# Key stage of a packed attention kernel: exponentials transposed by VectorE instead of TensorE, values loaded in long runs, the value products split into 32x32 tiles

## The chip, the cores and the metric

The kernel runs on one core of a Trainium2 chip. The metric is the device time of one execution in microseconds (us). Before the change the median of three runs was 1665.73 us (1664.1 to 1666.33). TensorE (PE) multiplies matrices into PSUM, VectorE (DVE), ScalarE (ACT) and GpSimd (POOL) do elementwise work, and SyncE (SP) issues all DMAs here. Each engine works through its own instructions in order and waits on semaphores.

## The reference, cut to what matters

```python
def sm_attn(qq, kk, vv):                      # scale = 1/sqrt(64)
    s = scale * np.matmul(qq, kk.transpose(0, 1, 3, 2))
    s = s - np.max(s, axis=-1, keepdims=True)
    a = np.exp(s)
    a = a / (np.sum(a, axis=-1, keepdims=True) + 1e-09)
    return np.matmul(a, vv)
p_packed = sm_attn(p, k, v)                   # p: (8, 8, 32, 64); k, v: (8, 8, 576, 64)
out = sm_attn(q, p_packed, p_packed)          # q: (8, 8, 576, 64)
x = out.transpose(0, 2, 1, 3).reshape(4608, 512)
# then RMS norm, a gated layer (512 -> 1536 -> 512) and a layer with g = h*cos(h) (512 -> 2048 -> 512)
```

For each of 8 batches and 8 heads, 32 latent rows p attend to 576 keys and values. Their result is the key and the value of a second attention, whose queries are q. The change lies in the first attention alone.

## The kernel before, in words

The first attention is called the key stage here. It takes 16 groups, one after the other: a group i is four heads of one batch, so 4 heads x 32 latents fill the 128 partitions. The loop over i (L621 to L672, 18 rounds) is written as a software pipeline, and its order is the engines' order: it stands under a manual schedule. In round i these helpers follow each other:

- `u_et(i-1)` transposes the exponentials of the group before: six TensorE transposes `et` (L431), two ScalarE copies to `eT` (L432), and on VectorE the sum's reciprocal (L434, L435).
- `u_s1(i)` multiplies latents and keys into the scores `s` (L404, from group 11 on L408); VectorE takes the maximum `mx` (L412) and scales it (L413).
- `u_prep(i+1)` transposes the next latents (`pt`, L376) and copies them to `pT` on VectorE (L377); `u_kt(i+1, ...)` transposes the next keys (`kp`, L389), copied by ScalarE to `kT` (L392).
- `u_fin(i-2)` transposes the result `cd` of two groups before (`tp`, L459), ScalarE copies it to `tf` (L461), VectorE writes `ppT` (L464).
- `u_e(i)` takes the exponentials `e` on ScalarE (L420).
- `w_prep(n, 0)` and later `w_late` narrow 64-bit float weights to 32 bits: an absolute value on ScalarE (L133) and then four VectorE operations (L143, L145, L149, L153) per weight tile; "the narrowing" below means these four. One or two tiles are due in a round. `wo_split` (L528, L531) divides such a tile into a high and a low part.
- `u_pp(i-1)` multiplies `eT` with the values `vn` into `pp` (L445, 24 products: six chunks of keys by four heads), and VectorE evicts them to `cd` (L449), scaled by the reciprocal. `cd` has two buffers; the stores of `cd` and `tf` go to DRAM at the start of the next round (`store`, L578).
- `bg0_step` drives pieces of the second attention of batch 0 from round 5 on (`qtp`, `sp`, `st`, `amx`, `at`, `xp`, `ssq`, `rp`), and `unit` (rounds 6, 10, 14) multiplies narrowed weights `wy` with `ppT` into `mps` (L565), split by `hilo` (L106, L107) into `wmhl`.

Keys come in one DMA for each group, with 4608 contiguous bytes for each partition, values in three (L360), each to 32 partitions, for each of these four heads with runs of 1536 bytes. `vn` has three buffers with a zeroed border (L336, L618); `e` has a border too (L339). After the loop the core goes over to the gated layer (`gv`, L158 to L160), whose first product waits for the pieces `apt` of the second attention.

Of the kernel before, what the change touches and what calls it, by code (L numbers as in the profile page):

```python
# [9 lines left out]
F32 = mybir.dt.float32  # L10
F32R = mybir.dt.float32r
I32 = mybir.dt.int32
AF = mybir.ActivationFunctionType
# [7 lines left out]
def kernel(  # L21
# [14 lines left out]
    nc = tc.nc  # L36
    B, H, S, D = q.shape
    NP = p.shape[2]
# [3 lines left out]
    CP = 96  # L42
    NC_ = S // CP
    HALF = S // 2
    CH = NC_ // 2
# [4 lines left out]
    NG = 2 * B  # L50
# [9 lines left out]
    BG_B, KP_B = 2, 4  # L60
    WO_U = 4
    REST = S - 512
    V_P = 16
    R_LOAD, R_SPLIT, S_AT = (1, 2), (4, 5), (20, 21, 24 + 1, 24 + 2)
    W_FROM, W_TO = 1, 16
    W_ORD = (0, 1, 2, 3, 16, 4, 5, 6, 17, 7, 8, 18, 9, 10, 11, 19, 12, 13, 14)
# [7 lines left out]
    B0_W = (15, 16, 17, 18, 19, -4, 20, 21, -5, 22, 23, -6, 0, -7, 0, -8, 0, -9, 0, -10, 0, -11)  # L74
    B0_L, B0_LEAD = {15: (0,), 16: (1, 2), 17: (3,)}, 4
    W_LOAD, W_SPLIT = (4, 6, 14, 16), (9, 11, 17, 19)
    W2_I0, W2_POOL = 28, False
    T_END, F3_B, OWN = 2, 3, 16
    LAG, LAG_B = 3, 4
# [12 lines left out]
    ident = const.tile([128, 128], F32, name="ident")  # L92
# [87 lines left out]
    u5 = ust.enter_context(tc.tile_pool(name="u5", bufs=4))  # L180
    u2 = ust.enter_context(tc.tile_pool(name="u2", bufs=2))
    u1 = ust.enter_context(tc.tile_pool(name="u1", bufs=1))
    ps_2 = pst.enter_context(tc.tile_pool(name="ps_2", bufs=KP_B, space=PSUM))
# [5 lines left out]
    pT = u1.tile([128, 4, 160], F32, name="pT")  # L189
# [22 lines left out]
    def att_load(b):  # L212
        nc.sync.dma_start(out=bq, in_=q_dram[b])
# [117 lines left out]
                fs[word[0]](int(word[1]), int(word[2]))  # L331
            yield nxt[:1]

    v_t = [u2.tile([128, 4, NC_, D], F32, tag=f"vn{x}", name="vn", bufs=1) for x in range(3)]
    for x in range(2):
        nc.vector.memset(v_t[x], 0.0)  # L336
    e_pad = u2.tile([128, 2 * V_P + S], F32, tag="e", name="e", bufs=1)
    for x in (slice(0, V_P), slice(V_P + S, 2 * V_P + S)):
        nc.vector.memset(e_pad[:, x], 0.0)  # L339
    nat_k, nat_v = {}, {}  # L340
    st = {}

# [10 lines left out]
    def load_v(i):  # L353
        if i >= NG:
            return
        b, g = divmod(i, 2)
        vn = nat_v[i] = v_t[i % len(v_t)]
        vs = v[b, 4 * g:4 * g + 4].rearrange("h (p m c) d -> m p h c d", m=CH, c=NC_)
        for m in (0, 2, 1):
            nc.sync.dma_start(out=vn[V_P + m * 32:V_P + (m + 1) * 32], in_=vs[m])  # L360

    load_k(0)
    for i in range(2):
# [7 lines left out]
    def u_prep(i):  # L371
        pn, kn = nat_k.pop(i)
        z = st[i] = {}
        nc.gpsimd.tensor_copy(pn[:, 1], pn[:, 0])
        pt = ps_2.tile([128, 128], F32, tag="kp", name="pt")
        nc.tensor.transpose(pt, pn.rearrange("p a d -> p (a d)"), ident)  # L376
        nc.vector.tensor_copy(pT[:, :, :NP], pt.rearrange("p (h n) -> p h n", h=4))  # L377
        z["kT"], z["kn"] = u1.tile([128, 4, HALF], F32, tag="kT", name="kT"), kn

    def u_kt(i, ms):  # L380

        z = st[i]
        kT, kn = z["kT"], z["kn"]
        kv = kT.rearrange("q h (t m p) -> q h t m p", t=CH, m=CH)
        for m in ms:
            kp = ps_2.tile([128, CH * 128], F32, tag="kp", name="kp")
            for t in range(CH):
                r = 2 * (CH * m + t)
                nc.tensor.transpose(  # L389
                    kp[:, t * 128:(t + 1) * 128], kn[:, r:r + 2, :].rearrange("p c d -> p (c d)"), ident  # L390
                )
            nc.scalar.activation(  # L392
                out=kv[:, :, :, m, :], in_=kp.rearrange("q (t h p) -> q h t p", t=CH, h=4), func=AF.Copy
            )

    def u_s1(i):
# [19 lines left out]
    def u_e(i):  # L416
        z = st[i]
        s1, mx = z["s1"], z["mx"]
        e = e_pad[:, V_P:V_P + S].rearrange("p (a s) -> p a s", a=2)
        nc.scalar.activation(  # L420
            out=e, in_=s1[:, :, :HALF], func=AF.Exp, scale=scale, bias=mx[:, 1:2], accum_out=mx[:, 2:3]
        )

    def u_et(i):
        z = st[i]
        eT = u2.tile([128, NC_, 128], F32, tag="eT", name="eT", bufs=1)
        for hf in range(2):
            et = ps_2.tile([128, CH, 128], F32, tag="kp", name="et")
            for c in range(CH):
                cc = hf * CH + c  # L430
                nc.tensor.transpose(et[:, c, :], e_pad[:, cc * CP:cc * CP + 128], ident)  # L431
            nc.scalar.activation(out=eT[:, hf * CH:(hf + 1) * CH], in_=et, func=AF.Copy)  # L432
        z["eT"], mx = eT, z["mx"]
        nc.vector.tensor_scalar(out=mx[:, 2:3], in0=mx[:, 2:3], scalar1=1e-9, scalar2=None, op0=ALU.add)  # L434
        nc.vector.reciprocal(out=mx[:, 3:4], in_=mx[:, 2:3])  # L435

    def u_pp(i):
        b, g = divmod(i, 2)
        z = st[i]
        eT, vn, mx = z["eT"], nat_v.pop(i), z["mx"]  # L440
        pp = ps_2.tile([128, D], F32, tag="kp", name="pp")
        for c in range(NC_):
            for h in range(4):
                r = slice(h * NP, (h + 1) * NP)
                nc.tensor.matmul(  # L445
                    pp[r], eT[:, c, r], vn[:, h, c % CH * 2 + c // CH, :], start=c == 0, stop=c == NC_ - 1
                )
        cd = u2.tile([128, 2, D], F32, tag="cd", name="cd", bufs=2)
        nc.vector.tensor_scalar(  # L449
            out=cd, in0=pp.unsqueeze(1).to_broadcast([128, 2, D]), scalar1=mx[:, 3:4], scalar2=None, op0=ALU.mult  # L450
        )
        stores.append((c_dram[b][:, g, :], cd[:, 0, :]))
        z["cd"] = cd

    def u_fin(i):
        z = st[i]
        b, g = divmod(i, 2)
        tp = ps_2.tile([128, 4, NP], F32, tag="kp", name="tp")
        nc.tensor.transpose(tp.rearrange("p h n -> p (h n)"), z["cd"].rearrange("p a d -> p (a d)"), ident)  # L459
        tf = u2.tile([128, 4, NP], F32, tag="tf", name="tf", bufs=3)  # L460
        nc.scalar.activation(out=tf, in_=tp, func=AF.Copy)  # L461
        stores.append((q_dram[b][:, 4 * g:4 * g + 4, :], tf))
        n, t = b % 4, ppT[b // 4]
        nc.vector.tensor_tensor(  # L464
            out=t[:, 4 * g:4 * g + 4, n * NP:(n + 1) * NP], in0=tp,
            in1=gT[:, 4 * g:4 * g + 4].unsqueeze(2).to_broadcast([128, 4, NP]), op=ALU.mult
        )
        st.pop(i)
# [4 lines left out]
    def w_load(n):  # L473
        if n >= W_KV:
            wo_load(n - W_KV)
            return
        wy_load(n)
# [57 lines left out]
    def b0_load(x):  # L535
        if x < len(B0_W) and B0_W[x]:
            n = B0_W[x]
            (wy_load if n >= 0 else wo_load)(abs(n))
# [36 lines left out]
    def store(keep):  # L575
        while len(stores) > keep:
            dst, src = stores.pop(0)
            nc.sync.dma_start(out=dst, in_=src)  # L578
# [23 lines left out]
    def w_due(i):  # L602
        a, b = (n_w * max(0, min(x, W_TO) - W_FROM) // (W_TO - W_FROM) for x in (i, i + 1))
        return [W_ORD[x] for x in range(a, b)]
# [10 lines left out]
    order.enter_context(tc.manual_schedule())  # L615
    u_prep(0)
    u_kt(0, range(CH))
    nc.gpsimd.memset(v_t[2], 0.0)  # L618
    w_q, wo_q = [], []
    w_late = lambda: None  # L620
    for i in range(NG + 2):  # L621
        due = list(w_due(i))
        for n in due:
            w_load(n)
        load_k(i + 4)
        for n in B0_L.get(i, ()):
            b0_load(n)
        if i == 1:
            load_q()
            load_q()  # L630
        store(0)
        if i == U_ATT:
            att_load(0)
            att_load_c(0)
        if 0 < i <= NG:
            u_et(i - 1)
        if i < NG:
            u_s1(i)
        if i + 1 < NG:
            u_prep(i + 1)  # L640
            u_kt(i + 1, [0, 1])
        if 1 < i:
            u_fin(i - 2)
        if i <= NG:
            w_late()
        if i < NG:
            u_e(i)
        if i + 1 < NG:
            u_kt(i + 1, [2])
        for n in w_q:  # L650
            w_prep(n, 0)
        for n in wo_q:
            wo_split(n - W_KV, 0)
        bg0_step(i, 1)
        if 0 < i <= NG:
            u_pp(i - 1)
        if i in U_S:
            unit(0, U_S[i])
        bg0_step(i, 0 if i == U_ATT else 2)
        w_last = w_late  # L660

        def w_late(ns=tuple(w_q), os=tuple(wo_q)):
            for n in ns:
                w_prep(n, 1)
            for n in os:
                wo_split(n - W_KV, 1)
        if i < NG:
            w_late()
            w_late = lambda: None
        wo_q = [n for n in w_q if n >= W_KV]  # L670
        w_q = due
        load_v(i + 2)  # L672
# [187 lines left out]
    for i in range(len(seq) + LAG):  # L860
        b, f, hf = seq[min(i, len(seq) - 1)]
        j = i - b * B1
        if i < len(seq):
# [11 lines left out]
            t = gv_block(b, hf, f)  # L875
# [137 lines left out]
    for i in range(len(seq) + LAG_B):  # L1013
        if i < len(seq):
            n, f = seq[i]
# [16 lines left out]
        if LAG_B <= i < len(seq) + LAG_B - T_END:  # L1032
            n, f = seq[i - LAG_B]
# [33 lines left out]
```

## Time and profile before

| What | Before |
|---|---|
| Median of 3 runs | 1665.73 us |
| Profiled execution, its own time | 1664.63 us |
| Its span (first to last instruction) | 1662.8 us |
| TensorE busy over the span | 1607.7 us (97%) |
| VectorE, ScalarE, GpSimd busy | 1006.9, 809.6, 74.9 us |
| Mean granted TensorE clock | 0.983 |

The span is cut by the page into 40 slices of 41.6 us. TensorE is busy 7, 7, 6 and 7 tenths in the first four and 9 or 8 tenths in every later one; the DMA engines are busy 9 tenths or more in the first three. The key stage is what fills these four slices: the first product of the gated layer starts at 155.63 us. In the profile a product of 32-bit floats shows as two records, so 24 products `pp` are 48 records.

### The profile page before, as it was taken

Reading aid. Unit: us, or ns where it says so; the run is one execution under the profiler, and the core shown is the slowest. Engines: PE = TensorE matmul, PEld = TensorE weight load, DVE = VectorE, ACT = ScalarE, POOL = GpSimd, SP = SyncE. Lnnn points to the kernel's source line nnn. Section 1 sums busy time; section 2 is a strip of 40 time slices with the busy share of each in tenths; the row PEclk is TensorE's granted clock in tenths of the full one; section 3 lists DMA queues with packets and bytes.
Section 4 is the critical chain, followed back from the end, with each engine's and each line's share of the span. In section 5 each row is a group of like instructions: output and inputs, shape, how many; then the busy total and the mean of one; then the engine's idle time right before and its main releaser. Section 6 shows DMA issues by size and latency. Waiting matters only on the chain.

```text
span 1662.8 us, 25654 instructions
## 1 busy us (share of the span) xinstructions
PE 1607.7 (97%) x9920; PEld 1308.2 (79%) x9920; DVE 1006.9 (61%) x1890; ACT 809.6 (49%) x1519; POOL 74.9 (5%) x74
## 2 busy tenths in 40 slices
PE   7767989999999999999999999999999999999998
PEld 5545768787888888888988888888888888888887
DVE  3567985666666656564426665656565656565554
ACT  3455554444454444443425555545454545454443
POOL 1000540000000000000210000000000000000000
PEclk9787999999999999999999999999999999999999
DMA  9996754454645453533372110101010101000001
GB/s 235 266 268 198 227 165 153 155 189 145 198 140 185 147 196 131 169 125 110 112 257 77 38 38 1 51 1 51 1 51 0 51 1 51 1 10 16 1 26 26
DMA packets 103577, 177.31 MB, mean 107 GB/s; under 512 B 39456, under 2 KB 55840, under 8 KB 103456
## 3 DMA queue, kind: packets, MB, share of 16 engines
q1 hardware_dynamic: 103456, 175.68, 34.9%
q8 instruction: 78, 1.28, 0.3%
q14 instruction: 43, 0.35, 0.1%
HBM read 134.22 MB, written 41.42 MB: 106 GB/s over the span
## 4 chain that ended last, share of the span: by engine, by line
PE 89%; DVE 4%; DMA 3%; ACT 1%; issue 1%; POOL 0%; SPq 0%; DVEq 0%; ACTq 0%; POOLq 0%
PE hp L159 8%; PE hp L160 8%; PE hp L158 8%; PE ops L160 8%; PE ops L159 8%; PE ops L158 8%; PE gv L158 6%; PE acc L158 6%; PE gv L159 6%; PE acc L160 6%; PE gv L160 6%; PE acc L159 6%; PE mps L565 3%; DMA c<-cd 2%; PE qtp L229 1%
## 5 line engine op out<-in xcount | busy, mean ns | idle before, releaser
L158 PE MATMUL gv<-apt,wmhl 128*128 128x288 f32 x768 | 234.0, 305 | 2.0 <-ACT apt L106 0.9
L159 PE MATMUL gv<-apt,wmhl 128*128 128x288 f32 x768 | 227.8, 297 | 0.4 <-DVE apt L107 0.4
L160 PE MATMUL gv<-apt,wmhl 128*128 128x288 f32 x768 | 226.8, 295 | 0.0
L159 PE MATMUL hp<-xhl,wmhl 128*128 128x512 f32 x576 | 224.1, 389 | 0.0
L160 PE MATMUL hp<-xhl,wmhl 128*128 128x512 f32 x576 | 224.1, 389 | 0.0
L158 PE MATMUL ops<-w2hl,ghl 128*128 128x512 f32 x576 | 224.1, 389 | 0.0
L159 PE MATMUL ops<-w2hl,ghl 128*128 128x512 f32 x576 | 224.1, 389 | 0.0
L158 PE MATMUL hp<-xhl,wmhl 128*128 128x512 f32 x576 | 223.9, 389 | 0.0
L160 PE MATMUL ops<-w2hl,ghl 128*128 128x512 f32 x576 | 222.3, 389 | 0.0
L966 ACT ACTIVATE r<-r 128x512 f32<-128x512 f32 x144 | 91.0, 632 | 250.0 <-DVE r L965 250.0
L974 DVE TENSOR_TENSOR r<-r,hp 128x512 f32<-128x512 f32 x144 | 98.9, 687 | 164.7 <-ACT r L967 164.7
L758 ACT ACTIVATE shl<-silu 128x288 fp32r<-128x288 f32 x192 | 85.4, 445 | 201.6 <-DVE silu L751 201.6
L158 PEld LDWEIGHTS gv<-apt,wmhl 128*128 128x128 f32 x768 | 145.0, 189 | 49.0 <-issue 15.3
L158 PE MATMUL acc<-shl,wohl 128*128 128x512 f32 x432 | 175.4, 406 | 1.1 <-ACT wohl L528 0.9
L160 PE MATMUL acc<-shl,wohl 128*128 128x512 f32 x432 | 170.4, 394 | 2.8 <-POOL wohl L531 2.8
L159 PE MATMUL acc<-shl,wohl 128*128 128x512 f32 x432 | 169.6, 393 | 0.0
L961 ACT ACTIVATE kk<-hp,magic 128x512 f32<-128x512 f32 x144 | 99.1, 688 | 117.4 <-PE hp L160 117.2
L751 DVE TENSOR_TENSOR silu<-silu,gv 128x288 f32<-128x288 f32 x192 | 86.4, 450 | 106.8 <-PE gv L160 81.9
L159 PEld LDWEIGHTS gv<-apt,wmhl 128*128 128x128 f32 x768 | 145.0, 189 | 5.9 <-DVE apt L107 0.6
L160 PEld LDWEIGHTS gv<-apt,wmhl 128*128 128x128 f32 x768 | 144.9, 189 | 0.0
L962 DVE TENSOR_SCALAR kk<-kk 128x512 f32<-128x512 f32 x144 | 61.4, 426 | 116.2 <-ACT kk L961 116.1
L159 PEld LDWEIGHTS ops<-w2hl,ghl 128*128 128x128 f32 x576 | 108.2, 188 | 22.6
(122 smaller groups left out, 2624.6 us busy)
## 6 DMA issues: line engine op xcount, KB each, us to landing
wy<-wy SPq DMA_DIRECT2D x96, 512.0 KB, 4.6
kn<-in_k_dram SPq DMA_DIRECT2D x16, 576.0 KB, 7.9
vn<-in_v_dram SPq DMA_DIRECT2D x48, 192.0 KB, 6.7
qnat<-in_q_dram SPq DMA_DIRECT2D x32, 288.0 KB, 4.1
x_dram<-x SPq DMA_DIRECT2D x18, 512.0 KB, 3.0
x1raw<-x_dram SPq DMA_DIRECT2D x18, 512.0 KB, 3.9
raw<-in_moe_w_in_dram SPq DMA_DIRECT2D x16, 512.0 KB, 4.3
raw<-in_moe_w_out_dram SPq DMA_DIRECT2D x16, 512.0 KB, 4.3
```

The costliest lines, as they stand in the source:

```text
L158: nc.tensor.matmul(ps, lhi, rhi, start=first, stop=False)
L159: nc.tensor.matmul(ps, lhi, rlo, start=False, stop=False)
L160: nc.tensor.matmul(ps, llo, rhi, start=False, stop=last)
L229: nc.tensor.transpose(tp[:, c * CP:(c + 1) * CP], qv[:, i, 2 * c:2 * c + 2, :].rearrange("p c d -> p (c d)"), ident[:CP, :CP],)
L565: nc.tensor.matmul(ps[kt][h * NP:(h + 1) * NP], ppT[b // 4][rows, 4 * kt + h, n:n + NP], w_y[2 * u + kt][rows, j], start=True, stop=True,)
L751: nc.vector.tensor_tensor(out=t, in0=t, in1=pss[1], op=ALU.mult)
L758: nc.scalar.activation(out=sh[:, 0, cols], in_=t, func=AF.Copy)
L961: nc.scalar.activation(out=kk, in_=hp, func=AF.Identity, scale=1.0 / TWO_PI, bias=magic[:, 0:1])
L962: nc.vector.tensor_scalar(out=kk, in0=kk, scalar1=-MAGIC, scalar2=None, op0=ALU.add)
L966: nc.scalar.activation(out=r, in_=r, func=AF.Abs)
L974: nc.vector.tensor_tensor(out=r, in0=r, in1=hp, op=ALU.mult)
```

## The change

Five things are changed, all in the key stage.

1. The exponentials are no longer transposed by TensorE with ScalarE copies: one VectorE instruction turns the 32x32 blocks of `e` into `eT`.
2. The order of keys within a group changes with it: `kT` takes the keys so that a chunk is 32 keys of one head in that head's 32 partitions. Values come in the layout of the keys: one DMA for each group, 128 partitions, 4608 contiguous bytes each; `vn` is an ordinary tile with four buffers (`VB`), and the zeroed borders and their memsets go.
3. The value products are 18 chunks by four heads, each with 32 rows and 32 columns of the array, on the diagonal, where there were six chunks by four with 128 rows.
4. The eviction of `pp` to `cd` leaves `u_pp` and becomes `u_cd`, which stands behind the narrowing at the round's end. `cd` and `tf` get four buffers.
5. The copy of the latents to `pT` moves from VectorE to ScalarE.

```diff
-        for m in (0, 2, 1):
-            nc.sync.dma_start(out=vn[V_P + m * 32:V_P + (m + 1) * 32], in_=vs[m])
+        vn = nat_v[i] = u5.tile([128, CH * NC_, D], F32, tag="vn", name="vn", bufs=VB)
+        nc.sync.dma_start(out=vn, in_=v[b, 4 * g:4 * g + 4].rearrange("h (p c) d -> (h p) c d", c=CH * NC_))
...
-        nc.vector.tensor_copy(pT[:, :, :NP], pt.rearrange("p (h n) -> p h n", h=4))
+        nc.scalar.activation(out=pT[:, :, :NP], in_=pt.rearrange("p (h n) -> p h n", h=4), func=AF.Copy)
...
-        kv = kT.rearrange("q h (t m p) -> q h t m p", t=CH, m=CH)
+        kv = kT.rearrange("q h (c p) -> q h c p", p=NP)
...
-        for hf in range(2):
-            et = ps_2.tile([128, CH, 128], F32, tag="kp", name="et")
-            for c in range(CH):
-                cc = hf * CH + c
-                nc.tensor.transpose(et[:, c, :], e_pad[:, cc * CP:cc * CP + 128], ident)
-            nc.scalar.activation(out=eT[:, hf * CH:(hf + 1) * CH], in_=et, func=AF.Copy)
+        eT = u2.tile([128, 2, HALF // NP, NP], F32, tag="eT", name="eT", bufs=1)
+        nc.vector.transpose(eT.rearrange("p a c n -> p (a c n)"), z["e"].rearrange("p a s -> p (a s)"))
...
-                    pp[r], eT[:, c, r], vn[:, h, c % CH * 2 + c // CH, :], start=c == 0, stop=c == NC_ - 1
+                    pp[r], eT[r, c % 2, c // 2], vn[r, c], start=c == 0, stop=c == n_c - 1
                 )
-        cd = u2.tile([128, 2, D], F32, tag="cd", name="cd", bufs=2)
+        z["pp"] = pp
+
+    def u_cd(i):
...
+        cd = u2.tile([128, 2, D], F32, tag="cd", name="cd", bufs=4)
...
-        tf = u2.tile([128, 4, NP], F32, tag="tf", name="tf", bufs=3)
+        tf = u2.tile([128, 4, NP], F32, tag="tf", name="tf", bufs=4)
...
         if i < NG:
             w_late()
             w_late = lambda: None
+        if 0 < i <= NG:
+            u_cd(i - 1)
```

VectorE, one early round before the change, from the reciprocal's two small operations to the end of the narrowing:

```order
L434 TENSOR_SCALAR mx<-mx 128x1
L435 RECIPROCAL mx<-mx 128x1
L412 TENSOR_REDUCE mx<-s_480 128x1
L413 TENSOR_SCALAR mx<-mx 128x1
L377 COPY pT<-pt 128x4x32
L464 TENSOR_TENSOR ppT_175<-tp,gT 128x4x32
L449 TENSOR_SCALAR cd<-pp,mx 128x128
L143 TENSOR_SCALAR wy<-wy 128x512
L145 TENSOR_SCALAR wy<-wy 128x512
L149 SCALAR_TENSOR_TENSOR wy<-wo,wy 128x512
L153 SCALAR_TENSOR_TENSOR wy<-wo,wy 128x512
```

The same round on VectorE after the change:

```order
L419 STREAM_TRANSPOSE eT<-e 128x576
L421 TENSOR_SCALAR mx<-mx 128x1
L422 RECIPROCAL mx<-mx 128x1
L404 TENSOR_REDUCE mx<-s_538 128x1
L405 TENSOR_SCALAR mx<-mx 128x1
L457 TENSOR_TENSOR ppT_175<-tp,gT 128x4x32
L143 TENSOR_SCALAR wy<-wy 128x512
L145 TENSOR_SCALAR wy<-wy 128x512
L149 SCALAR_TENSOR_TENSOR wy<-wo,wy 128x512
L153 SCALAR_TENSOR_TENSOR wy<-wo,wy 128x512
L442 TENSOR_SCALAR cd<-pp,mx 128x128
```

The eviction `cd` has moved from ahead of the narrowing to behind it, the turn of `e` stands at the head of the round, and the copy to `pT` is gone from this engine.

TensorE, one round before the change, from the scores to the next scores:

```order
L404 MATMUL s_578<-kT,pT 128x288 x8
L376 MATMUL pt<-ident,pn 128x128
L389 MATMUL kp<-ident,kn 128x128 x6
L459 MATMUL tp<-ident,cd 128x128
L389 MATMUL kp<-ident,kn 128x128 x3
L445 MATMUL pp<-vn,eT 32x64 x24
L431 MATMUL et<-ident,e 128x128 x6
L404 MATMUL s_675<-kT,pT 128x288 x8
```

The same round on TensorE after the change:

```order
L396 MATMUL s_675<-kT,pT 128x288 x8
L368 MATMUL pt<-ident,pn 128x128
L381 MATMUL kp<-ident,kn 128x128 x6
L452 MATMUL tp<-ident,cd 128x128
L381 MATMUL kp<-ident,kn 128x128 x3
L432 MATMUL pp<-vn,eT 32x64 x72
L396 MATMUL s_811<-kT,pT 128x288 x8
```

The six transposes between the products and the next scores are gone, and the products are three times as many.

VectorE at the end of the loop before the change, from the last narrowing operation of round 15 to the first piece of `apt`:

```order
L153 SCALAR_TENSOR_TENSOR wy<-wo,wy 128x512
L531 TENSOR_TENSOR wohl<-ny,wohl 128x512
L434 TENSOR_SCALAR mx<-mx 128x1
L435 RECIPROCAL mx<-mx 128x1
L464 TENSOR_TENSOR ppT_176<-tp,gT 128x4x32
L449 TENSOR_SCALAR cd<-pp,mx 128x128
L464 TENSOR_TENSOR ppT_176<-tp,gT 128x4x32
L107 TENSOR_TENSOR apt<-at,apt 128x576 x2
```

The same place after the change:

```order
L153 SCALAR_TENSOR_TENSOR wy<-wo,wy 128x512
L524 TENSOR_TENSOR wohl<-ny,wohl 128x512
L442 TENSOR_SCALAR cd<-pp,mx 128x128
L419 STREAM_TRANSPOSE eT<-e 128x576
L421 TENSOR_SCALAR mx<-mx 128x1
L422 RECIPROCAL mx<-mx 128x1
L457 TENSOR_TENSOR ppT_176<-tp,gT 128x4x32
L442 TENSOR_SCALAR cd<-pp,mx 128x128
L457 TENSOR_TENSOR ppT_176<-tp,gT 128x4x32
L107 TENSOR_TENSOR apt<-at,apt 128x576 x2
```

Between the last narrowing and the last `cd` there now stand the eviction of the group before and the turn of the last group's exponentials, on which the last group's products wait.

## Rows read from the trace of the kernel before

**Rows 1.** Chain of waits, 0 to 157 us, shares by line.

```profile
by line: DMA c<-cd 22.5%; PE s L404 7.3%; PE kp L389 4.6%; PE et L431 3.8%; issue 3.6%; DVE wy L149 3.6%; DVE wy L153 3.5%; ACT e L420 3.1%; ACT kT L392 2.9%; DVE mx L412 2.9%; DMA q<-tf 2.8%; DMA kn<-in_k_dram 2.6%; DVE wy L145 2.5%; DVE w
```

**Rows 2.** One source line: the 16 maxima of L412 (min/median/max ns).

```profile
L412 DVE TENSOR_REDUCE mx<-s x16: 736/740/759, 12.4 to 148.2; 128x1 f32<-128x576 f32 x16
```

**Rows 3.** One source line: what ended the idle time before L449 (us, times).

```profile
  DMA c<-cd: 21.5, 6
```

**Rows 4.** Timeline of VectorE: start us, us, instruction [idle before <-releaser].

```profile
39.48 0.35 DVE L449 TENSOR_SCALAR cd<-pp,mx 128x128 f32<-128x128 f32 x1 [8.20 <-DMA c<-cd]
...
47.82 0.35 DVE L449 TENSOR_SCALAR cd<-pp,mx 128x128 f32<-128x128 f32 x1 [4.24 <-DMA c<-cd]
...
55.42 0.35 DVE L449 TENSOR_SCALAR cd<-pp,mx 128x128 f32<-128x128 f32 x1 [3.50 <-DMA c<-cd]
...
64.45 0.35 DVE L449 TENSOR_SCALAR cd<-pp,mx 128x128 f32<-128x128 f32 x1 [2.48 <-DMA c<-cd]
...
66.90 1.29 DVE L107 TENSOR_TENSOR wmhl<-mps,wmhl 128x512 fp32r<-128x512 f32 x2 [2.10 <-ACT wmhl L106]
...
73.28 0.76 DVE L412 TENSOR_REDUCE mx<-s 128x1 f32<-128x576 f32 x1 [1.98 <-PE s L404]
...
84.50 0.35 DVE L449 TENSOR_SCALAR cd<-pp,mx 128x128 f32<-128x128 f32 x1 [2.39 <-PE pp L445]
...
91.89 0.35 DVE L449 TENSOR_SCALAR cd<-pp,mx 128x128 f32<-128x128 f32 x1 [0.63 <-DMA c<-cd]
...
103.35 0.35 DVE L449 TENSOR_SCALAR cd<-pp,mx 128x128 f32<-128x128 f32 x1 [2.48 <-DMA c<-cd]
```

**Rows 5.** Timeline of ScalarE, same columns.

```profile
35.55 0.66 ACT L133 ACTIVATE wy<-wo 128x512 f32<-128x512 f32 x1 [3.49 <-DMA wo<-in_moe_w_gate_dram]
...
44.32 0.66 ACT L133 ACTIVATE wy<-wo 128x512 f32<-128x512 f32 x1
...
52.66 0.68 ACT L133 ACTIVATE wy<-wo 128x512 f32<-128x512 f32 x1
...
82.84 0.66 ACT L133 ACTIVATE wy<-wo 128x512 f32<-128x512 f32 x1
...
101.54 1.09 ACT L106 ACTIVATE wmhl<-mps 128x512 fp32r<-128x512 f32 x2
```

**Rows 6.** Groups of instructions, 0 to 300 us: count | busy us, mean ns | idle.

```profile
L565 PE MATMUL mps<-wy,ppT 64*32 64x512 f32 x208 | 17.9, 632 | 5.5 <-ACT qT L233 4.7 <-DVE wy L153 0.9
...
L377 DVE COPY pT<-pt 128x128 f32<-128x128 f32 x16 | 4.5, 281 | 0.0
...
L276 DVE STREAM_TRANSPOSE at<-s 128x576 f32<-128x576 f32 x4 | 3.1, 767 | 0.0
```

**Rows 7.** Timeline of TensorE: one product group, one group of transposes.

```profile
68.78 1.49 PE L431 MATMUL et<-ident,e 128*128 128x128 f32 x6
...
75.60 0.88 PE L445 MATMUL pp<-vn,eT 128*32 128x64 f32 x48
```

**Rows 8.** Timeline of VectorE at the end of the key stage.

```profile
152.92 0.68 DVE L531 TENSOR_TENSOR wohl<-ny,wohl 128x512 fp32r<-128x512 f32 x1
...
153.97 0.34 DVE L449 TENSOR_SCALAR cd<-pp,mx 128x128 f32<-128x128 f32 x1
```

**Rows 9.** Timeline of TensorE at the end of the key stage.

```profile
151.59 1.51 PE L445 MATMUL pp<-vn,eT 128*32 128x64 f32 x48
...
155.63 0.40 PE L158 MATMUL gv<-apt,wmhl 128*128 128x288 f32 x1 [0.94 <-ACT apt L106]
```

**Rows 10.** Windows: stretch, length, busy by engine, PEclk, DMA share, GB/s.

```profile
36.00:40.00 4.00, 0.11 (x1) 0.12 (x2) 0.52 (x2) 0.97 (x3) 0.24 (x1) 0.72 1.10 190
...
104.00:108.00 4.00, 3.64 (x58) 2.88 (x57) 3.86 (x9) 1.15 (x3) 0.29 (x1) 0.50 1.03 348
...
150.00:153.60 3.60, 2.97 (x55) 2.40 (x55) 2.83 (x6) 3.28 (x8) 0.00 (x0) 0.56 0.90 285
```

**Rows 11.** DMA issues of the page: count, KB each, us to landing.

```profile
vn<-in_v_dram SPq DMA_DIRECT2D x48, 192.0 KB, 6.7
```

More of the change, by code (lines that the diff above doesn't have):

```diff
@@ L62 @@
     REST = S - 512
-    V_P = 16
     R_LOAD, R_SPLIT, S_AT = (1, 2), (4, 5), (20, 21, 24 + 1, 24 + 2)
@@ L76 @@
     W_LOAD, W_SPLIT = (4, 6, 14, 16), (9, 11, 17, 19)
+    VB = 4
     W2_I0, W2_POOL = 28, False
@@ L332, in attend @@
             yield nxt[:1]
[L334 to L339, printed above, removed]
     nat_k, nat_v = {}, {}
@@ L356, in load_v @@
         b, g = divmod(i, 2)
-        vn = nat_v[i] = v_t[i % len(v_t)]
-        vs = v[b, 4 * g:4 * g + 4].rearrange("h (p m c) d -> m p h c d", m=CH, c=NC_)
-        for m in (0, 2, 1):
-            nc.sync.dma_start(out=vn[V_P + m * 32:V_P + (m + 1) * 32], in_=vs[m])
+        vn = nat_v[i] = u5.tile([128, CH * NC_, D], F32, tag="vn", name="vn", bufs=VB)
+        nc.sync.dma_start(out=vn, in_=v[b, 4 * g:4 * g + 4].rearrange("h (p c) d -> (h p) c d", c=CH * NC_))
     load_k(0)
@@ L392, in u_kt @@
             nc.scalar.activation(
-                out=kv[:, :, :, m, :], in_=kp.rearrange("q (t h p) -> q h t p", t=CH, h=4), func=AF.Copy
+                out=kv[:, :, CH * m:CH * (m + 1), :], in_=kp.rearrange("q (t h p) -> q h t p", t=CH, h=4), func=AF.Copy
             )
@@ L418, in u_e @@
         s1, mx = z["s1"], z["mx"]
-        e = e_pad[:, V_P:V_P + S].rearrange("p (a s) -> p a s", a=2)
+        e = z["e"] = u2.tile([128, 2, HALF], F32, tag="e", name="e", bufs=1)
         nc.scalar.activation(
@@ L425, in u_et @@
         z = st[i]
-        eT = u2.tile([128, NC_, 128], F32, tag="eT", name="eT", bufs=1)
-        for hf in range(2):
-            et = ps_2.tile([128, CH, 128], F32, tag="kp", name="et")
-            for c in range(CH):
-                cc = hf * CH + c
-                nc.tensor.transpose(et[:, c, :], e_pad[:, cc * CP:cc * CP + 128], ident)
-            nc.scalar.activation(out=eT[:, hf * CH:(hf + 1) * CH], in_=et, func=AF.Copy)
+        eT = u2.tile([128, 2, HALF // NP, NP], F32, tag="eT", name="eT", bufs=1)
+        nc.vector.transpose(eT.rearrange("p a c n -> p (a c n)"), z["e"].rearrange("p a s -> p (a s)"))
         z["eT"], mx = eT, z["mx"]
@@ L437, in u_pp @@
     def u_pp(i):
-        b, g = divmod(i, 2)
         z = st[i]
-        eT, vn, mx = z["eT"], nat_v.pop(i), z["mx"]
+        eT, vn = z["eT"], nat_v.pop(i)
         pp = ps_2.tile([128, D], F32, tag="kp", name="pp")
-        for c in range(NC_):
+        n_c = CH * NC_
+        for c in range(n_c):
             for h in range(4):
@@ L445, in u_pp @@
                 nc.tensor.matmul(
-                    pp[r], eT[:, c, r], vn[:, h, c % CH * 2 + c // CH, :], start=c == 0, stop=c == NC_ - 1
+                    pp[r], eT[r, c % 2, c // 2], vn[r, c], start=c == 0, stop=c == n_c - 1
                 )
-        cd = u2.tile([128, 2, D], F32, tag="cd", name="cd", bufs=2)
+        z["pp"] = pp
+    def u_cd(i):
+        b, g = divmod(i, 2)
+        z = st[i]
+        pp, mx = z["pp"], z["mx"]
+        cd = u2.tile([128, 2, D], F32, tag="cd", name="cd", bufs=4)
         nc.vector.tensor_scalar(
@@ L617 @@
     u_kt(0, range(CH))
-    nc.gpsimd.memset(v_t[2], 0.0)
     w_q, wo_q = [], []
```

## The prediction

> **What bounds the kernel now.** TensorE is busy nearly all the time from 155.63 us on, where the gated layer starts [rows 9]; the change touches nothing behind that point. So I read the key stage alone. First comes the chain of waits: 22.5% of the stretch stands under the store of `cd`, 35 us by the chain's reckoning [rows 1]. That is the store's whole flight, not what the engines lost. The line that waits, the eviction L449, shows the loss: VectorE sat idle before it for 21.5 us, in six waits for an earlier store to free one of two buffers [rows 3]. The timeline gives each wait, and what else was late there. The reader is to see two things: VectorE's order is the round's pace (its 16 maxima lie 135.8 us apart in 15 rounds, 9.05 us each [rows 2]), and behind a wait for a store there often stands another, for ScalarE or for weights, nearly as late [rows 4, 5]. The DMA engines are full besides, a share of 1.10 at 36 us and 1.03 at 104 us [rows 10].
>
> **First term, the waits that go.** With four `cd` buffers, and the eviction behind the narrowing, nothing in front of the narrowing waits for a store. What comes next decides the gain, and this is `wy` on ScalarE, which the narrowing needs. The narrowing begins some 0.3 us after an eviction starts (0.35, overlapped).
> - Wait of 8.20: `wy` ended at 35.55 + 0.66 = 36.2, the narrowing began near 39.8, so 3.5 us. But `wy` itself waited 3.49 for its weights. They come sooner if the value loads ahead of them take less; then up to 6.9. I take 6.0, near the upper end, because some four value loads stand ahead of these weights.
> - Wait of 4.24: 48.1 against 44.32 + 0.66 + 0.1 = 45.1: 3.0.
> - Wait of 3.50: 55.7 against 53.4: 2.3.
> - First wait of 2.48: nothing, since the next instruction waits 2.10 for ScalarE's `wmhl`.
> - The wait of 2.39 for the products `pp` at 84.50 goes too, as the narrowing no longer stands behind `cd`: 84.8 against 83.6, 1.2.
> - 0.63: 0.6. Second wait of 2.48: `wmhl` could start near 102.1 instead of 103.6, when the first half of ScalarE's pair is done: 1.5.
>
> In sum 14.6 us off, between 12.1 (weights no sooner) and 15.5 [rows 4, 5].
>
> **Second term, a longer round on VectorE.** Each round gains a turn of 128x576, as L276 does it in 0.77, and loses the copy to `pT`, 0.28 [rows 6]. Where both lie on VectorE's chain that is +0.49 a round. In rounds in which `cd` and the copy stood inside a wait (for a store, or for ScalarE), they cost nothing before; now the eviction lies on the chain, 0.3 us between the narrowing and the next maximum, and the price comes to 1.0. I take 0.6, nearer to the lower end, because rounds bound by other waits hide a part. 14 rounds by 0.6 are 8.4. One round is another matter: the maximum at 73.28 waited 1.98 for the scores [rows 4], and ahead of these scores stood six transposes of 1.49 [rows 7], which go; under that wait VectorE's addition is free and about 1.1 is won. Net 7.3 us on, between 5.8 (14 x 0.49 less 1.1) and 14.0 (14 x 1.0).
>
> TensorE's part is hidden elsewhere: three times as many products, by the row of 0.88 for a group at most 2.6, less up to 1.49 for the transposes [rows 7]; the products need a turn of the round before, and run while VectorE takes the maximum. If that cover went (the array at its lower level, 1.51 x 3 = 4.5), a round in which the scores are late would pay 2 to 3 us. ScalarE loses two copies and gains a small one, and it waited in most rounds. The value loads' saved time is set at zero beyond the weights above, because no wait in rows 3 to 5 ends with a value load.
>
> **Third term, the end of the stage.** Here the change adds a wait. Before, the last products (from 151.59) were done when VectorE reached their eviction at 153.97; `gv` began 1.66 us later [rows 8, 9]. Now VectorE comes out of `wohl` at 152.92 + 0.6 = 153.5, evicts the group before (0.3), turns the last exponentials (0.77), and only then can the last products start, near 154.6. [...] The eviction lands at 157.2 to 159.1 instead of 153.97. Behind that waiting eviction VectorE has the pieces `apt` and two narrowings queued, and TensorE the gated layer. So 3.2 to 5.1 us on; a group of products has a fixed tail that is not tripled, so I allow 2.9 at the low end and take 3.8.
>
> **Sum.** -14.6 + 7.3 + 3.8 = -3.5 us. The profiled execution took 1664.63 us (span 1662.8), 1.1 less than the median of the runs, so 1661.1 for such an execution and 1662.2 for a median. With all bounds together the sum lies between -6.8 and +7.0. What a measurement here can tell from no change is about 0.2%, 3.3 us: my value stands on that border.
>
> **Rivals.**
>
> *The DMA engines pace the rounds, and the values' long runs set them free.* For it: shares over 1 through most of the stage. Two windows with like shares moved 190 and 348 GB/s [rows 10]. All values, 48 loads of 192 KB [rows 11], are 9.4 MB: 49.7 us at the one rate, 27.1 at the other, 22.6 apart at most. Some 13 of 16 groups load while the queue is full, so 18.4, less 3.8 at the end and 2.7 for three late rounds that DMA doesn't pace: -11.9, or 1653.8. Against it: only one of the waits I read ends with a load. [...]
>
> *VectorE's round grows by the full price (the other side).* Place: between the narrowing and the next maximum, in every round, where the eviction and the turn now stand in series with the weights' work. Price 1.0 us in 14 rounds, 14.0, with the end at 5.1, against 12.1 of waits: +7.0, 1672.7. It decides from about 0.85 us a round (14.6 - 3.8 + 1.1 over 14). For it: VectorE already sets the pace, and in the later rounds no wait for a store is left to pay with. Against it: those later rounds also wait for ScalarE, so some of it hides.
>
> *The small products run one after another.* Then a group costs 2.6 x 4 = 10.6 instead of 2.6. A round can't be shorter than its products alone, 1.5 above the 9.05 of now: 15 x 1.5 = 23 at the least, and 10.6 - 0.88 = 9.7 at the end, so 1698 or more. Against it: `mps` has 64-row halves that write parts of the same PSUM tile, and 208 records of 632 ns fit into 17.9 us busy, some seven at a time [rows 6]. [...]
>
> *The change does nothing that counts:* the store's wait is replaced by the one for weights, as DMA stays as full as it is, and term 1 shrinks to what terms 2 and 3 take. 1665.7.
>
> **Chances.** Forecast 0.50 (own range 1658.5 to 1667), DMA sets the rounds free 0.22, VectorE's full price 0.18, products in series 0.04, nothing 0.06. Faster by over 0.2%: 0.27 of the forecast's half and 0.22, together 0.49. Within 0.2%: 0.23, 0.06 and 0.06, together 0.35. Slower: 0.12 and 0.04, together 0.16. The range runs from 1652, which takes in most of the DMA case, to 1669, which takes in the milder half of VectorE's.
>
> **What would show it.** Right: the eviction line has no wait for a store; the fourth to seventh maximum come 1.5 to 6 us sooner after one another, and the tenth some 8 to 10 us sooner than before; the late rounds are 0.5 to 1.0 longer; `gv` starts 3 to 4 us before 155.63, with VectorE idle for 2 to 5 us before its last eviction. Product groups of 2.0 to 2.6 us at full clock would confirm that the tiles run together; 8 us or more would be the third rival. A mean DMA share clearly under 1 from 40 us on, with rounds still as long, would say that VectorE sets the pace; late rounds that shrink would say DMA. I am wrong if `gv` starts after 156 us, or before 148.

## The result and the profile after

The changed kernel took 1683.84 us in the median (1679.57 to 1687.07) against 1665.89 beside it: a ratio of 1.0114, 95% interval 1.0093 to 1.0134. The forecast was a small gain; it became 18 us of loss. The profiled execution took 1682.97 us, with a span of 1681.2.

Most of it lies ahead of the gated layer: `gv` starts at 171.68 where it started at 155.63 [rows 9], 16.05 of the profiled execution's 18.3 us (the 2.3 behind it were not followed up). Lines have moved: the products are L432 now, the scores L396, the keys' transposes L381, the latents' turn L452, the eviction L442, the maximum L404. First TensorE's timeline at the end, then VectorE's (start us, us, instruction, idle before and releaser), then the maxima, all of the changed kernel.

```profile
166.76 3.06 PE L432 MATMUL pp<-vn,eT 32*32 32x64 f32 x144 [0.35 <-DVE mx L421]
...
171.68 0.61 PE L158 MATMUL gv<-apt,wmhl 128*128 128x288 f32 x1 [0.94 <-ACT apt L106]
```

```profile
165.07 0.69 DVE L524 TENSOR_TENSOR wohl<-ny,wohl 128x512 fp32r<-128x512 f32 x1
...
169.87 0.35 DVE L442 TENSOR_SCALAR cd<-pp,mx 128x128 f32<-128x128 f32 x1 [2.74 <-PE pp L432]
```

```profile
L404 DVE TENSOR_REDUCE mx<-s x16: 737/740/759, 12.8 to 160.4; 128x1 f32<-128x576 f32 x16
```

The maxima span 147.6 us for 135.8 [rows 2]. The loss is not even. The fourth maximum comes at 40.6 instead of 29.6, 10.9 late; the eleventh at 100.4 instead of 98.4, only 2.0 late; the last is 12.2 late. What the change was to remove it did remove: what ended the idle time before L442 holds no store any more, where L449 had 21.5 us of them [rows 3].

```profile
  PE pp L432: 8.2, 4
```

What was lost shows in TensorE's timeline of the first rounds of the changed kernel:

```profile
19.79 1.90 PE L432 MATMUL pp<-vn,eT 32*32 32x64 f32 x123
21.62 2.20 PE L396 MATMUL s<-kT,pT 64*128 64x288 f32 x14
26.95 0.64 PE L396 MATMUL s<-kT,pT 64*128 64x288 f32 x2 [3.13 <-issue]
27.52 0.33 PE L368 MATMUL pt<-ident,pn 128*128 128x128 f32 x1
27.69 1.20 PE L381 MATMUL kp<-ident,kn 128*128 128x128 f32 x6
28.68 0.42 PE L452 MATMUL tp<-ident,cd 128*128 128x128 f32 x1
28.89 0.85 PE L381 MATMUL kp<-ident,kn 128*128 128x128 f32 x3
29.67 2.66 PE L432 MATMUL pp<-vn,eT 32*32 32x64 f32 x114
35.29 1.07 PE L432 MATMUL pp<-vn,eT 32*32 32x64 f32 x30 [2.96 <-issue]
36.29 4.21 PE L396 MATMUL s<-kT,pT 64*128 64x288 f32 x16
...
42.35 2.21 PE L432 MATMUL pp<-vn,eT 32*32 32x64 f32 x144
```

TensorE stops after 14 of 16 scores, and again after 114 of 144 product records, in the midst of work whose operands lie ready. Nothing in the profile releases it: "issue". Between the stops are 2 + 1 + 6 + 1 + 3 + 114 = 127 matmuls, each with its weight load, so 254 instructions. And with both stops the granted clock is down for a while (0.50 from 28.0 to 31.4 us and from 34.8 to 41.6): 16 scores take 4.21 us in the second of these stretches, 2.21 at a clock of 1.00.

The groups of TensorE from 0 to `gv` (busy us, mean ns | idle before) say how much there was of both:

```profile
L432 PE MATMUL pp<-vn,eT 32*32 32x64 f32 x2304 | 47.3, 246 | 10.1 <-issue 9.4 <-DVE mx L421 0.6
L396 PE MATMUL s<-kT,pT 64*128 64x288 f32 x176 | 30.6, 484 | 6.9 <-issue 4.9 <-ACT kT L384 1.9
```

Before, the same stretch had these products (L445):

```profile
L445 PE MATMUL pp<-vn,eT 128*32 128x64 f32 x768 | 16.2, 239 | 3.1 <-DVE pT L377 1.8 <-issue 1.4
```

So 14.3 us of idle time at "issue" against 1.4, and 31 us more of busy time on the products. Which of the two cost the time is what the experiments had to settle. A last view, the DMA queues (packets, MB, share) of the stretch up to `gv`: first the changed kernel, then before, and last the changed kernel between 23.8 and 24.6 us, within the first stop.

```profile
q8 instruction: 22, 0.36, 0.9%
```

```profile
q8 instruction: 11, 0.18, 0.5%
```

```profile
q8 instruction: 1, 0.02, 8.5%
```

Instructions come by DMA, in packets of 16 KB (0.36 MB over 22). In the whole kernel the packets of this queue go with TensorE's matmuls and weight loads: 78 for 19,840 before and 89 for 22,720 after, 254 and 255 a packet. The changed stage needs twice as many, as it has 2,885 matmuls ahead of `gv` and the kernel before 1,444: at 127 a packet, 22.7 and 11.4 packets. One comes in each of the first two stops, and none in the 5 us between them. The stops end with it: by the trace's records the packets run from 24.40 to 25.49 and from 32.39 to 33.92 us, and TensorE goes on 1.5 and 1.4 us later. At the next two stops, which end at 53.63 and 62.01 us, packets end 1.2 to 1.3 us earlier (52.38 and 60.77).

### The profile page after: what moved, and what is told of

Same layout as the page of the kernel before. It is cut to its first block, busy times and chain, and to the rows that moved or that the text cites. A ratio compares the mean times of both kernels' runs of the same rounds, so it can differ in the third digit from the quotient of the medians.

```text
span 1681.2 us, 28454 instructions
## 1 busy us (share of the span) xinstructions
PE 1625.3 (97%) x11360; PEld 1330.2 (79%) x11360; DVE 1011.8 (60%) x1886; ACT 800.6 (48%) x1503; POOL 74.2 (4%) x73
## 4 chain that ended last, share of the span: by engine, by line
PE 91%; DVE 3%; DMA 2%; issue 2%; ACT 1%; POOL 0%; SPq 0%; DVEq 0%; POOLq 0%; ACTq 0%
PE hp L158 8%; PE ops L158 8%; PE ops L160 8%; PE hp L160 8%; PE hp L159 8%; PE ops L159 8%; PE gv L158 6%; PE acc L158 6%; PE gv L159 6%; PE acc L160 6%; PE gv L160 6%; PE acc L159 6%; PE mps L558 3%; PE pp L432 2%; PE s L396 1%
```

## The experiments

Two theories. **Fetch:** the program of TensorE is longer by 90 matmuls and 90 weight loads a group (96 of each for the products, less the six transposes), and TensorE stops when the next packet of instructions is late. **Work:** the products simply take TensorE longer, in a place where that isn't hidden. Other suspects were the late eviction and the DMA engines. Ratios are to the kernel before, with their 95% interval; times of `gv`, like all views, are from one profiled execution each. Executions of one kernel lie up to 17 us apart, so a difference of a few us in `gv` alone says little.

**The eviction back behind the products** (the changed kernel otherwise).

```diff
         z["pp"] = pp
+        u_cd(i)
...
-        if 0 < i <= NG:
-            u_cd(i - 1)
```

> The changed kernel with one part undone: the eviction of pp to cd stands right behind the products again, ahead of the narrowing; all else stays. Three theories for the 18 us lost. L, the late eviction: the transpose tp, which TensorE has ahead of the last keys, the products and the next scores, waits for the eviction, so TensorE and SP stand still until the narrowing is done; undoing it gives 8 to 14 us back, to 1670 to 1676, and TensorE's idle time ahead of tp (17.8 us, 8 times) falls under 5 us. F, instruction fetch: TensorE's program is longer by 48 products a group and it idles at 'issue'; then the time stays at 1680 to 1686 and the issue gaps (9.4 us ahead of pp, 4.9 us ahead of s) stay. V, the turn on VectorE (0.77 us a round): also 1680 to 1686.

Measured: 1688.8 us, ratio 1.0134 [1.0109, 1.0159], `gv` at 179.4. The loss is not from the late eviction; without it the median is higher by 5 us, though the two intervals overlap. Idle time at "issue" comes to 30.5 us here (21.5 ahead of products, 6.3 of scores, 2.7 elsewhere). One row warns of how this is read:

```profile
50.86 1.24 PE L396 MATMUL s<-kT,pT 64*128 64x288 f32 x7 [2.91 <-issue]
57.32 0.76 PE L432 MATMUL pp<-vn,eT 32*32 32x64 f32 x39 [2.01 <-issue]
63.82 2.21 PE L432 MATMUL pp<-vn,eT 32*32 32x64 f32 x144 [2.00 <-issue]
```

The first two stand in the midst of a group, before the last 7 scores and the last 39 records of the products, as at 53.63 and 62.01 us in the changed kernel. The third stands ahead of a whole group: that may be a wait that the profile could not name. Idle time inside a group, at a place where all its operands have landed, is the safer sign. By it about half of the 30.5 us are stops, much as in the changed kernel, whose eight all stand inside a group.

**24 products a group**, over all 128 rows (heads mixed, two thirds of the keys left out).

```diff
-        n_c = CH * NC_
+        n_c = NC_
...
-                    pp[r], eT[r, c % 2, c // 2], vn[r, c], start=...
+                    pp[r], eT[:, c % 2, c // 2], vn[:, c], start=...
```

> The changed kernel with 24 value products a group instead of 72: six chunks by four heads over all 128 rows, as many as before. They mix the heads and leave two thirds of the keys out, so pp is not the reference's; loads, turn and late eviction stay. F: the issue gaps of TensorE in the key stage (some 14 us on the matmul side) fall under 4 us, mx of group 3 starts near 31 instead of 40.6 us, and the time falls by 10 to 14 us, to 1670 to 1674. L: the gaps go too or not, but the products are shorter by 1.3 to 2.5 us in rounds that wait for them, so only 3 to 6 us, 1678 to 1681. V: 1680 to 1686.

Measured: 1659.17 us, 0.9957 [0.9944, 0.9971], `gv` at 149.6, 11 instruction packets by then. No stop stands ahead of a matmul of the products or the scores:

```profile
L396 PE MATMUL s<-kT,pT 64*128 64x288 f32 x176 | 27.7, 460 | 7.3 <-ACT kT L384 7.2
...
L432 PE MATMUL pp<-vn,eT 128*32 128x64 f32 x768 | 18.7, 262 | 0.6 <-DVE mx L421 0.4
```

All other parts of the change are in, and it gains. The 48 added products a group are worth 24.7 us of the changed kernel's time, more than the 10 to 14 expected. The first two edits together:

> Both edits together: eviction in place and 24 products (sums as in the one before not the reference's). If F and L are separate causes their gains add: 1655 to 1664, below the kernel before. If they are one cause seen twice, the time is that of the better one alone, 1668 to 1674. V: still above 1676.

Measured: 1658.7 us, 0.9964 [0.9943, 0.9984]: the place of the eviction decides nothing once the products are few. This kernel too shows 12.3 us at "issue" ahead of products, but all five times ahead of a whole group, as in the third row above. So not every "issue" is a late packet.

**The kernel before with its products cut in three**, 72 a group over the same columns.

```diff
+        for d in (slice(0, 22), slice(22, 43), slice(43, D)):
           for c in range(NC_):
...
-                    pp[r], eT[:, c, r], vn[:, h, ..., :], ...
+                    pp[r, d], eT[:, c, r], vn[:, h, ..., d], ...
```

> The kernel before with 72 value products a group instead of 24, by cutting the 64 columns of each into 22, 21 and 21; columns, sums, loads and evictions stay. F: TensorE's issue gaps ahead of pp and s grow by 6 us or more, and the time rises by 6 to 14 us, 1672 to 1680. L and V: nothing but the products' own longer time, hidden beside the waits for stores: 1665 to 1668.

Measured: 1694.32 us, 1.0171 [1.0146, 1.0196], some 28 us more where theory F expected 6 to 14; `gv` at 186.1, 30.4 us late. Nothing else of the change is in it. Its products:

```profile
L446 PE MATMUL pp<-vn,eT 128*32 128x21 f32 (+1 forms) x2304 | 26.1, 195 | 23.9 <-issue 23.4 <-ACT eT L432 0.5
```

10 us more of busy time, and 28.8 us at "issue" (5.4 ahead of scores; those ahead of products all stand inside a group). So a longer program alone costs more than the whole change did.

**Fewer loads:** keys, values and latents of the changed kernel loaded for four groups only and used again.

```diff
+        if i >= 4:
+            nat_k[i] = kept_k[i % 4]
+            return
...
+        if i >= 4:
+            nat_v[i] = kept_v[i % 4]
+            return
```

> The changed kernel, with keys, values and latents loaded for the first four groups alone and used again by the later twelve (the packed attention of these groups isn't the reference's); 72 products, late eviction, all weight loads stay. Two readings of TensorE's issue gaps. F1, the fetch of its instructions queues behind other DMAs: with some 14 MB less to load the gaps ahead of pp and s in the key stage fall from 14 us to under 4, and the time to 1666 or less. F2, each piece of program costs a fixed gap whatever else is loaded: the gaps stay over 10 us and the time at 1676 or more.

Measured: 1671.23 us, 1.0038 [1.0022, 1.0054], `gv` at 157.0; the stops fell from 14.3 to 9.1 us, with a DMA share of 0.53 up to `gv` in place of 0.74. Both numbers lie between the theories: with fewer loads the stops are shorter, but they don't vanish. The time fell by more than they did (12.6 us); where the rest came from was not followed up.

**Four buffers in the kernel before**, and the same with the eviction behind the narrowing.

```diff
-        cd = u2.tile([128, 2, D], F32, tag="cd", name="cd", bufs=2)
+        cd = u2.tile([128, 2, D], F32, tag="cd", name="cd", bufs=4)
...
-        tf = u2.tile([128, 4, NP], F32, tag="tf", name="tf", bufs=3)
+        tf = u2.tile([128, 4, NP], F32, tag="tf", name="tf", bufs=4)
```

> The kernel before with four buffers for cd and four for tf, and nothing else. My first term says that the waits for stores (21.5 us) are worth 12 to 15 us, and there is no longer turn and no longer program: 1651 to 1656. A rival, that DMA (share over 1 in this stage) paces the rounds: 1661 to 1666, with the waits turned into waits for weights on ScalarE.

> As the one before, with the eviction moved behind the narrowing. The late eviction gained 5 us with 72 products and nothing with 24, so it should be within 2 us of the one before with in-place eviction; if TensorE's tp waits for it (as in the changed kernel, 17.8 us of idle time), 3 to 6 us slower than that.

Measured: 1662.15 us, 0.9988 [0.9971, 1.0006], and 1662.32, 0.9993 [0.9977, 1.0009]. The waits for stores are gone, yet the time hardly moves: both intervals take in no change. (The profiled execution of the first is one of its faster ones, 1659.34 us.) The first one's L449, and its DMA queue up to `gv` (149.1 us):

```profile
  PE pp L445: 4.6, 6
```

```profile
q1 hardware_dynamic: 22896, 38.09, 96.6%
```

The DMA engines stay full, and ScalarE's waits for weights grow from 3.5 to 8.5 us up to `gv`. That was the forecast's DMA rival.

**Long runs of the values in the kernel before** (loaded as in the changed kernel, so that they no longer match their weights).

```diff
-        vn = nat_v[i] = v_t[i % len(v_t)]
...
+        vn = nat_v[i] = u5.tile([128, CH * NC_, D], F32, tag="vn", name="vn", bufs=4)
+        nc.sync.dma_start(out=vn, in_=v[...].rearrange("h (p c) d -> (h p) c d", c=CH * NC_))
```

> The kernel before with the values loaded as in the changed one (one DMA a group, 128 partitions, 4608-byte runs, four buffers, no memsets); the 24 products then multiply the wrong values, so the sums aren't the reference's. If DMA is the pace, the gain is up to 18 us, 1648 to 1656, and the waits for stores shrink because the queue is shorter; if VectorE's order is, 1662 to 1666, and the waits stay within a third of 21.5 us.

Measured: 1650.9 us, 0.9914 [0.9895, 0.9932], `gv` at 141.4. Two `cd` buffers remain, and still no wait for a store is left. With the long runs come a fourth `vn` buffer and the loss of the memsets, which this run doesn't part from them. Its queue up to `gv`:

```profile
q1 hardware_dynamic: 18269, 38.08, 84.2%
```

84.2% of 141.4 is 119 us of the engines' time, against 95.4% of 155.6 = 148 before, for the same 38 MB.

**Work against fetch, by a cross.** Two kernels part the count of products from their columns. The first has 24 products over the columns of 72; the second the columns of 24 in 72 products.

```diff
-        pp = ps_2.tile([128, D], F32, tag="kp", name="pp")
-        n_c = CH * NC_
+        pp = ps_2.tile([128, CH, D], F32, tag="kp", name="pp")
+        n_c = NC_
...
-                    pp[r], eT[r, c % 2, c // 2], vn[r, c], start=...
+                    pp[r], eT[r, c % 2, c // 2], vn[r, CH * c:CH * (c + 1)], start=...
```

> The changed kernel with 24 products a group in place of 72, over the same 32 rows and the same columns in all: each takes three of the value blocks at once, 192 columns (its output keeps one third of the sums). The instructions are those of the 24-product run, the streaming that of the changed kernel. Theory F (what costs is that TensorE's program is longer and has to be fetched): no idle time of kind issue ahead of the products, 1658 to 1665 us. Theory T (what costs is TensorE's own time on the products, 47.3 us up to gv in the changed kernel and 18.7 us with 24 products): the products take over 35 us and the time is 1674 us or more.

```diff
-        n_c = CH * NC_
+        n_c = NC_
+        for d in (slice(0, 22), slice(22, 43), slice(43, D)):
           for c in range(n_c):
...
-                    pp[r], eT[:, c % 2, c // 2], vn[:, c], start=...
+                    pp[r, d], eT[:, c % 2, c // 2], vn[:, c, d], start=...
```

> The 24-product run with each product cut into three of 22, 21 and 21 columns: 72 instructions a group again, with the columns of 24 (heads mixed and two thirds of the keys left out, as there). Theory F: issue gaps of 10 us or more ahead of products and scores come back, 1672 us or more. Theory T: products of some 26 us up to gv (as the 72 thin ones of the earlier run took) against 18.7, so 1660 to 1667 us.

| products a group | columns of 24 | columns of 72 |
|---|---|---|
| 24 | 1659.17 us, `gv` 149.6 | 1664.74 us, `gv` 154.8, 1.0001 [0.9987, 1.0014] |
| 72 | 1684.77 us, `gv` 174.3, 1.0131 [1.0109, 1.0153] | 1683.84 us, `gv` 171.7 |

Three times the columns cost 5.6 us in the upper row and nothing in the lower; three times the instructions cost 19 to 26. (The kernels of the left column use all 128 rows for a product, those of the right 32.) The wide products, then the thin ones, each up to `gv`:

```profile
L432 PE MATMUL pp<-vn,eT 32*32 32x192 f32 x768 | 44.9, 391 | 0.6 <-DVE mx L421 0.4
```

```profile
L433 PE MATMUL pp<-vn,eT 128*32 128x21 f32 (+1 forms) x2304 | 29.9, 206 | 18.1 <-issue 17.6 <-DVE mx L421 0.4
```

With 44.9 us on the products and no stop, `gv` is 5.2 us later than with 18.7; with 29.9 and 24.3 us of stops (17.6 ahead of products, 5.6 of scores, 1.1 elsewhere) it is 24.7 later. And the thin products stop in the same places as the changed kernel's:

```profile
20.70 2.21 PE L396 MATMUL s<-kT,pT 64*128 64x288 f32 x14
26.74 0.64 PE L396 MATMUL s<-kT,pT 64*128 64x288 f32 x2 [3.83 <-issue]
...
29.85 1.48 PE L433 MATMUL pp<-vn,eT 128*32 128x22 f32 x114
34.13 0.63 PE L433 MATMUL pp<-vn,eT 128*32 128x21 f32 x30 [2.80 <-issue]
```

After 14 scores and after 114 product records, though the products are another size and the time another. So the place in the program sets the stop, not what is computed there. The wide kernel's stretch from 20 to 40 us, then the changed kernel's (PE busy and count, other engines, then granted clock, DMA share, GB/s), show the double price, idle time and a lower clock, while DMA was fuller in the one that never stopped:

```profile
20.00:40.00 20.00, 19.68 (x269) 14.22 (x263) 11.98 (x31) 9.73 (x27) 1.11 (x2) 1.00 1.05 308
```

```profile
20.00:40.00 20.00, 13.91 (x310) 10.86 (x299) 5.91 (x15) 4.04 (x11) 0.71 (x3) 0.78 0.88 224
```

**A version that keeps 24 products.** The values of the kernel before come in one load over 96 rows in place of three over 32; runs stay 1,536 bytes, and the keys' eviction writes in the order that this needs. The second run adds the four buffers.

```diff
-        for m in (0, 2, 1):
-            nc.sync.dma_start(out=vn[V_P + m * 32:V_P + (m + 1) * 32], in_=vs[m])
+        nc.sync.dma_start(out=vn[V_P:V_P + 96], in_=v[...].rearrange("h (p c) d -> p h c d", c=NC_))
...
-        kv = kT.rearrange("q h (t m p) -> q h t m p", t=CH, m=CH)
+        kv = kT.rearrange("q h (t p m) -> q h t m p", t=CH, m=CH)
```

> The kernel before with a group's values in one load over 96 rows in place of three over 32 rows each; the runs stay 1,536 bytes, the keys' eviction writes in the order that this needs. Theory D (what the change's long runs gained came from the length of the runs): 1663 to 1668 us. [...]

> The run before this one with four buffers for the evicted products and for the latents' copies. Theory D: as four buffers alone, 1660 to 1664 us. [...]

Measured: 1660.33 us, 0.9982 [0.9968, 0.9997], `gv` at 150.9; and 1659.79, 0.9981 [0.9962, 0.9999], `gv` at 144.7 (in the fastest of its executions, 1654.88 us). Both beat the kernel before, by some 3 us by their ratios (the intervals end just under 1), and the changed one by 23. The first lies 2.7 us under theory D's range, the second 0.2 under. The DMA engines' time up to `gv` fell, in the first, to 92.2% of 150.9 = 139 us: of the 29 us that the long runs save, some 9 come with the single load over 96 rows, and the rest with the longer runs or with 128 rows, which no run parts. One price was not expected, here the keys' eviction of the second run, then of the kernel before (min/median/max ns):

```profile
L390 ACT ACTIVATE kT<-kp x48: 660/686/731, 6.4 to 130.6; 128x384 f32<-128x384 f32 x48
```

```profile
L392 ACT ACTIVATE kT<-kp x48: 480/491/512, 6.3 to 141.6; 128x384 f32<-128x384 f32 x48
```

Writing every third element costs ScalarE 195 ns more, 9.4 us over 48.

## Why the prediction was wrong

**The step that failed** is in the second term: "TensorE's part is hidden elsewhere". It priced the 72 products of a group by their duration alone, at most 2.6 us, and found them covered. As duration they nearly were: three times the columns cost 5.6 us at most (the cross's upper row). But each product also is four instructions (two matmuls, each with its weight load), which come in the 16 KB packets, and this had no term at all. It measured 19 us between the wide kernel and the changed one (1664.74 to 1683.84; `gv` 16.9 later, with 14.3 us of stops), and 28.5 in the kernel before. The profile had the number for it, the queue of instructions with 11 packets up to `gv`: one in 14 us, which the change made one in 8. In the early rounds it is one in some 4 us, by an estimate (171 matmuls a round after the change, 127 a packet, and 5.6 us a round from the second to the fourth maximum before); measured, the 127 matmuls between the first two stops took 5.4 us. There, from 20 to 40 us, the DMA share was 1.08 before and 0.88 after, and there 11 us were lost by the fourth maximum. The kernel before even had one such stop, inside a group:

```profile
83.96 0.49 PE L445 MATMUL pp<-vn,eT 128*32 128x64 f32 x18 [1.35 <-issue]
```

The prediction met its trace as the wait of 2.39 for the products at 84.50 [rows 4], and did not ask what held the products up.

**First term, -14.6.** The reason was wrong, and that the size comes near a measured one is luck. The values' long runs alone gave -14 us; four buffers alone removed the same waits and gave -2, with the late eviction -1, neither told from no change. The waits for stores were the sign of full DMA engines (95.4% up to `gv` before, 96.6% with four buffers), not the cause of the time. The forecast set the loads' saved time "at zero beyond the weights"; its DMA rival had this right.

**Second and third term, +7.3 and +3.8.** The kernel with 24 products bears them out: up to the eleventh maximum it is 12.4 us faster than before (73.6 for 86.0), and its last five rounds are longer by 3.8 (53.7 for 49.8), 0.77 each, between the 0.5 and 1.0 named. In the changed kernel itself they are longer by 10.1 (60.0), 2.0 each, beyond what was named. Against the long runs alone its `gv` is 8.2 later, for 11.1 forecast. Its ratio of 0.9957 is -7 us, for a sum of -3.5 that still held tripled products at the end. In the changed kernel the last eviction ends 4.5 us after `wohl` does (165.76 to 170.22), within the 3.7 to 5.6 forecast. For the last products that forecast has 2.6 to 4.5 us, three times 0.88 and 1.51 [rows 7, 9]; they took 3.06, at a mean granted clock of 0.69. The tail that is not tripled shows at a clock of 1.00: 144 records took 2.21 us (42.35), not three times 0.88.

**The rivals.** Small products in series: no. 144 records took 2.2 us at a granted clock of 1.00 (42.35, 2.21) and not the 10.6 of that rival, so the four row tiles, which write one PSUM tile, did not wait for one another. VectorE's full price has the sign, but not the cause: the kernel with 24 products has all of VectorE's additions and gains 7 us. "I am wrong if `gv` starts after 156 us" came true, at 171.68.

**Still open:** what makes a packet come late. Fewer loads shortened the stops, but with a DMA share of 1.05 the wide kernel had none, so a full engine alone doesn't do it; the rate at which TensorE uses up its instructions has to be high too. The packets' records bear this out, if matmuls are counted in steps of 127 from the place of the first stop. The first two of these packets began 4.5 and 5.4 us after TensorE had entered the step before (19.91 to 24.40, 26.95 to 32.39) in the changed kernel, and 3.7 and 3.5 us after it in the wide one (20.30 to 24.01, 30.61 to 34.13). So they came late in both, but a step took the wide kernel 10.3 and 9.6 us, and the changed one 3.9 up to the first stop and 5.4 from there to the second. What sets a packet off, and what it waits for on the way, no run shows.

## What to carry to other kernels

Count an engine's instructions beside their time: where a change cuts one matmul into several, the instructions a microsecond in the busiest stretch, and the packets of the instruction queue there, belong in the sum (here three times the products cost 19 to 28 us). Idle time at "issue" inside a group of like instructions, at the same place in the program whatever their size, was the sign here that they came late (after 14 scores and after 114 records, with products of 64 columns and of 21 or 22). And a wait for a buffer that a store frees may only show that the DMA engines are full: here more buffers removed 21.5 us of waits and not the time (0.9988).

## What the runs showed of the hardware

- TensorE's instructions arrived in 16 KB packets over a queue of their own (q8: 22 packets, 0.36 MB, up to `gv` in the changed kernel); in the worst case a stop lasted 5.94 us (the kernel before with 72 products), ahead of the last 18 records of a group. In the first four stops of the changed kernel TensorE went on 1.2 to 1.5 us after a packet's end.
- With the stops went a lower clock: from 20 to 40 us the granted clock was 0.78 in the changed kernel, which stopped twice there, and 1.00 in the wide one, which did not stop.
- 48 loads of 32 rows in runs of 1,536 bytes held the DMA engines some 29 us longer up to `gv` (148 for 119) than 16 loads of 128 rows in runs of 4,608 bytes, for the same 38 MB.
- 32-row products with 192 columns took 44.9 us up to `gv`, those with 64 columns 47.3 for the same columns in all, but with 10.1 us of idle time ahead of them in place of 0.6: what the small ones lost was the wait for instructions, not the array's time.
